# Idle matmuls in TensorE's planned waits, in a planned long convolution and feed-forward kernel

## The chip, the cores and the metric

The kernel runs on one core of one Trainium2 chip. The metric is the device time of one execution in microseconds; the time of a kernel is the median over its runs.

## The reference

The inputs are one batch of 2048 positions with 640 channels. The work is a pre-norm block of two parts: a long convolution (over all 2048 positions, by Fourier transforms) that is gated by the normalised input, and a gated feed-forward of width 1728.

```python
k_shift = sum over t of k_pad[:, t:t + S, :] * shift_k[:, ks - 1 - t]     # 4 taps
kv = k_shift * v
y = irfft(rfft(kv padded to 2S) * rfft(ssm_k padded to 2S))[:S]
y = y + kv * ssm_D
h = x + layernorm(x) * y
h2 = h + (silu(layernorm(h) @ w_gate) * (layernorm(h) @ w_up)) @ w_down
```

`x` is the input `A_q`; all inputs are bfloat16.

## The kernel before

The positions are cut into four blocks `j` of 512. The convolution over 2048 positions becomes block products in a transformed domain: the product for block `j` takes the spectra of value blocks 0 to `j` and of kernel blocks `j` to 0. The channels are cut into two halves `c` of 320. Block 0 uses one dense transform (`dense_c`, line 869): for each of four parts `h` it runs four-step accumulations of 320 columns (`dense_h`), products on VectorE, and eight inverse matmuls into accumulators. Blocks 1 to 3 (`conv_c`, line 1192) use a two-stage transform: `fwd` (line 831) with tables, an SBUF to SBUF shuffle by DMA, `spec` (line 903) with two matmuls of 64 loaded columns[...], products, `inv2`, another shuffle, and a last stage in `conv_bp`. The normalised result is transposed (`ln_bp`, line 1208, matmuls at line 1223) and feeds the feed-forward: `ffn_f` (line 1262) with matmuls of 512 columns, `ffn_b` (line 1284) for the projection down. Transposes of the convolution's kernel are in `k_turn` (line 810), whose first operation is named `ktr00`.

The order of the work is not written by hand. Each operation is an `Op` with a cost per engine; `schedule` (line 255) lays all of them out on a timeline once, in Python, before the program is built. It takes costs from small formulas, such as `mm_c` (line 669) for matmuls and `act_c` and `dve1` for evictions, and priorities from a long list. It also keeps a model of the TensorE clock (`pe_end`, line 180). What it yields for an operation is its engine, its place in the engine's order, and a planned `start` and `finish`. Every operation of an engine is issued in that order.

`emit` (line 367) turns the plan into programs. For each operation it collects the semaphores that it has to wait for, leaves out those already waited for, and appends the waits and then the instructions: "w" is a wait, "f" an instruction without a signal, "i" one with a signal.[...]

PSUM has eight slots of 512 float32 columns[...]: three in the pool `pF` (feed-forward, and in the convolution of block 0 one of the two pairs of accumulators, and some of the taps), five in `pC` (all else). `poolbases` holds their first columns and `seq` the tiles of a pool in the order of the program; a tile's `touch` lists the operations that write or read it, the eviction among them. Evictions are at lines 677 and 680 on ScalarE and lines 678 and 681 on VectorE. Nearly all matmuls are recorded at the helper line 694; VectorE's products and sums are recorded at line 913. Transfers are issued by SyncE (SP) at line 685 and, for accumulating ones, by GpSimd at line 1089.

## Time and profile before

| what | value |
|---|---|
| median of 6 runs | 298.28 us |
| lowest and highest run | 297.25 and 300.76 us |
| time of the profiled execution | 298.61 us |
| its span | 296.8 us |
| mean granted TensorE clock in it | 0.994 |
| TensorE busy | 281.6 us, 95% of the span, 1807 instructions |
| TensorE weight loads busy | 154.2 us, 52%, 1826 instructions |
| VectorE busy | 240.2 us, 81%, 491 instructions |
| ScalarE busy | 196.5 us, 66%, 472 instructions |
| GpSimd busy | 25.7 us, 9%, 31 instructions |

The span is what the hardware profiler saw of the program from the first instruction to the last; the execution's own time is a little longer. Matmuls are pipelined: a record goes on after the next matmul has started, and its end is modelled, so a busy TensorE need not be at its peak. In the 40 slices each digit is the busy share of a slice in tenths, and PEclk is the granted clock in tenths. In the views of waits a line names who waited for whom, then the total in us, the number of times and the longest. In views in order of time a line gives the start and the length in us, then engine, line and operation, how many are merged in it, and in brackets the idle time of the engine ahead of it and what ended it.

### The profile page before, as it was taken

The page shows a single profiled execution, that of the slowest core. Times are in us where ns is not written, and L with a number is a line of the kernel's source. Part 1 is how long each engine was busy: PE and PEld are TensorE (multiplying, and loading weights), DVE is VectorE, ACT ScalarE, POOL GpSimd, SP SyncE. Part 2 cuts the span into 40 slices and gives each one's busy share as a digit, 9 for nine tenths or more (in the row PEclk, how much of TensorE's full clock was granted, in tenths as well). Part 3 has the DMA queues.
Part 4 walks back from the last instruction along what each step waited for, and adds up shares of the span by engine and source line. Part 5 has one row for each costly group of instructions (what it writes and reads, how often), then busy time and mean ns, then how long its engine had stood idle before and what let it go on. Part 6 is the DMA issues. An engine that isn't in the chain of part 4 may idle for free.

```text
span 296.8 us, 5194 instructions
## 1 busy us (share of the span) xinstructions
PE 281.6 (95%) x1807; PEld 154.2 (52%) x1826; DVE 240.2 (81%) x491; ACT 196.5 (66%) x472; POOL 25.7 (9%) x31
## 2 busy tenths in 40 slices
PE   8889988897989999999999999999999999999996
PEld 2466654543534466564444557644444675444574
DVE  4799999999899899999999999994899932304322
ACT  4378899976968968977898995777885131341000
POOL 2000200103111022101101203000010010000000
PEclk9999999799999999999999999999999999999999
DMA  7999997915763787747806007844202033000002
GB/s 220 350 382 315 315 355 253 306 66 156 229 122 114 203 172 215 200 164 177 214 3 176 25 21 200 156 135 154 70 0 79 12 84 93 2 0 0 2 0 88
DMA packets 44050, 43.24 MB, mean 146 GB/s; under 512 B 14895, under 2 KB 38889, under 8 KB 43898
## 3 DMA queue, kind: packets, MB, share of 16 engines
q1 hardware_dynamic: 40168, 38.63, 41.7%
q0 software_dynamic: 3328, 3.97, 8.5%
q10 hardware_dynamic: 530, 0.33, 0.4%
q8 instruction: 14, 0.23, 0.3%
q14 instruction: 10, 0.08, 0.1%
HBM read 20.63 MB, written 2.62 MB: 78 GB/s over the span
## 4 chain that ended last, share of the span: by engine, by line
PE 78%; DVE 15%; DMA 3%; issue 2%; ACT 1%; SPq 1%
PE ps L694 76%; DVE sb L913 12%; DMA sb<-sb 1%; DMA sb<-in_A_q_dram 1%; DVE stt L1003 1%; DVE sb L678 1%; PE ps L1223 1%; SPq L685 1%; ACT sb L677 1%; DVE sb L1028 0%; ACT sb L1249 0%; PE ps L823 0%; DVE sb L681 0%; ACT sb L1042 0%; DVE stt L1007 0%
## 5 line engine op out<-in xcount | busy, mean ns | idle before, releaser
L694 PE MATMUL ps<-sb 128*128 128x320 bf16 (+1 forms) x1207 | 226.2, 339 | 6.3 <-DVE sb L913 2.1
L913 DVE TENSOR_TENSOR sb<-sb 128x1280 bf16<-128x1280 bf16 (+3 forms) x286 | 171.5, 657 | 3.7 <-ACT sb L677 2.7
L694 PEld LDWEIGHTS ps<-sb 128*128 128x128 bf16 (+1 forms) x1226 | 116.4, 98 | 99.5 <-issue 9.6
L677 ACT ACTIVATE sb<-ps 128x320 bf16<-128x320 f32 (+1 forms) x277 | 110.5, 477 | 29.4 <-PE ps L694 22.4
L694 PE MATMUL ps<-sb,tab 128*128 128x320 bf16 (+2 forms) x512 | 64.7, 306 | 5.8 <-issue 1.7
L913 DVE TENSOR_TENSOR sb<-ps,sb 128x512 bf16<-128x512 f32 (+2 forms) x46 | 28.2, 618 | 39.9 <-PE ps L694 28.8
L1249 ACT ACTIVATE sb<-ps 128x512 bf16<-128x512 f32 (+1 forms) x56 | 33.3, 598 | 35.9 <-PE ps L694 35.5
L694 PEld LDWEIGHTS ps<-sb,tab 128*128 128x128 f16 (+2 forms) x512 | 31.7, 101 | 37.5 <-issue 12.4
L1029 ACT ACTIVATE sb<-sb,stt 128x320 bf16<-128x320 bf16 (+1 forms) x27 | 19.6, 761 | 9.3 <-DVE stt L1021 6.6
L1019 POOL TENSOR_TENSOR stt<-stt 128x2 f32<-128x2 f32 (+1 forms) x12 | 12.2, 1024 | 114.5 <-DVE stt L1018 110.1
L1089 POOL DMA_DIRECT2D sb<-sb x12 | 12.2, 1016 | 97.0 <-DVE sb L913 68.5
L680 ACT ACTIVATE sb<-ps 128x320 bf16<-128x320 f32 x46 | 17.6, 449 | 2.6 <-PE ps L694 2.3
L678 DVE CAST sb<-ps 128x320 bf16<-128x320 f32 x32 | 15.0, 479 | 4.5 <-PE ps L694 4.2
L1003 DVE BATCH_NORM_STATS2 stt<-sb 128x6 f32<-128x320 bf16 x32 | 14.3, 474 | 0.1
L1049 ACT ACTIVATE sb<-sb,stt 128x640 bf16<-128x640 bf16 x16 | 13.3, 832 | 0.8 <-DVE stt L1045 0.8
L1042 ACT ACTIVATE sb<-sb 128x640 bf16<-128x640 bf16 x16 | 11.9, 746 | 0.5 <-DMA sb<-in_A_q_dram 0.4
L681 DVE TENSOR_SCALAR sb<-ps 128x320 bf16<-128x320 f32 x10 | 4.8, 484 | 3.5 <-PE ps L694 3.4
L1028 DVE TENSOR_SCALAR sb<-sb,stt 128x320 bf16<-128x320 bf16 (+1 forms) x21 | 7.4, 374 | 0.0
L823 PEld LDWEIGHTS ps<-sb 128*128 128x128 bf16 (+1 forms) x48 | 3.3, 121 | 1.7 <-issue 1.2
L823 PE MATMUL ps<-sb 128*128 128x128 bf16 (+1 forms) x48 | 3.8, 227 | 0.3 <-ACT sb L677 0.3
L1223 PE MATMUL ps<-sb 128*128 128x128 bf16 x40 | 3.8, 243 | 0.0
L1223 PEld LDWEIGHTS ps<-sb 128*128 128x128 bf16 x40 | 3.3, 111 | 0.6
(24 smaller groups left out, 22.7 us busy)
## 6 DMA issues: line engine op xcount, KB each, us to landing
sb<-sb SPq DMA_DIRECT2D x72, 160.0 KB, 2.2
sb<-sb POOLq DMA_DIRECT2D x12, 320.0 KB, 4.4
out_dram<-sb SPq DMA_DIRECT2D x16, 160.0 KB, 2.1
sb<-in_A_k_dram SPq DMA_DIRECT2D x8, 280.0 KB, 4.6
sb<-in_B_w_down_dram SPq DMA_DIRECT2D x13, 160.0 KB, 4.4
sb<-cst_den SPq DMA_DIRECT2D x8, 256.0 KB, 6.6
sb<-in_A_q_dram SPq DMA_DIRECT2D x6, 320.0 KB, 3.7
sb<-in_A_v_dram SPq DMA_DIRECT2D x6, 320.0 KB, 3.4
```

The costliest lines, as they stand in the source:

```text
L677: fns = {"act": lambda a: a.activation(out=dst(), in_=src(), func=ACTF.Copy), "dve": lambda v: v.tensor_copy(out=dst(), in_=src())}
L678: "dve": lambda v: v.tensor_copy(out=dst(), in_=src())}
L680: fns = {"act": lambda a: a.activation(out=dst(), in_=src(), func=ACTF.Copy, scale=scale), "dve": lambda v: v.tensor_scalar(out=dst(), in0 ...
L694: return lambda t: t.matmul(o(), l(), r(), start=st, stop=sp)
L913: return lambda v: v.tensor_tensor(out=o(), in0=a(), in1=b_(), op=op)
L1003: vec(dve1(CW, False), lambda v: v.bn_stats(st6(l, j, b, c), V(xt, b * D + c * CW, CW)), [(xt, (b, c))], [(ST, ("s", l, j, b, c))], prio, ...
L1019: P.op({"pool": 0.75}, lambda g: g.tensor_tensor(out=y, in0=va, in1=stt[:, 420:420 + hi - lo], op=ALU.pow), c1 + [(ST, "half")], c3, prio, ...
L1029: "act": lambda a: a.activation(out=dst(), in_=src(), func=ACTF.Identity, scale=rs(l, j, b), bias=tmv(l, j, 3)[:, b:b + 1])},
L1042: P.op({"act": act_c(D) + 0.22}, lambda a, b=b, jt=jt: a.activation(out=V(jt, 0, D), in_=V(xt, b * D, D), func=ACTF.Copy, accum_out=tmv(l, ...
L1049: P.op({"act": act_c(D) + 0.3}, lambda a, b=b, jt=jt: a.activation(out=V(jt, 0, D), in_=V(xt, b * D, D), func=ACTF.Square, bias=tmv(l, j, ...
L1089: P.op({"pool": 1.35}, [lambda g: g.dma_start(v4(t0), src(), accum_op=ALU.add)], [(t0, 0)] + cells, [(t0, 0)], prio, dma=(2.1, 2.1, 0.8), ...
L1249: P.op({"act": act_c(n)}, lambda a: a.activation(out=dst(), in_=src(), func=ACTF.Silu), rd, wr, -1000, name=f"si{nm}", after=after)
```

## The change

`Prog` gets a new function, `fill`. For an operation `o` of TensorE it looks at the wait that the plan leaves between the end of the operation before, `busy`, and `o.start`. It acts only where the planned start lies between 9 and 62 us and the planned wait is longer than 0.25 us. It goes through all slots of `pF` and `pC`, leaves out a slot whose tile begins with `o`, and takes for the others the tile that was begun last before `o`; from the end of the plan's last operation on that tile (plus 0.14 us) or of `busy`, whichever is later, to `o.start` it counts a free stretch, less 0.12 us. The slot with the longest free stretch is taken, and the number of matmuls is 0.6 of that stretch over 0.0557 us.

`emit` puts the result into TensorE's program ahead of `o`'s own waits: first waits for those operations on the slot's last tile that other engines do, as far as they were not waited for already; then so many matmuls of the 128x128 identity with itself, 128 columns, into the first 128 columns of the slot. Nothing reads what they write, and they signal nothing. It begins after the first operation of `k_turn`. The plan, the order of the operations on every engine, and all transfers stay as they are.

```diff
+    def fill(self, o, busy):
+
+        best = None
+        if 9.0 < o.start < 62.0 and o.start - busy > 0.25:
+            for pn in ("pF", "pC"):
+                for base in self.poolbases[pn]:
+                    ts = [t for t in self.pools[pn].seq if t.base == base and t.touch[0].start < o.start]
+                    prev = max(ts, key=lambda t: t.touch[0].start).touch if ts else []
+                    g = o.start - max([busy] + [p.finish + 0.14 for p in prev]) - 0.12
+                    if any(t.touch[0] is o for t in self.pools[pn].seq if t.base == base):
+                        continue
+                    if g > 0.12 and (best is None or g > best[2]):
+                        best = base, prev, g
+        return best and (best[0], best[1], int(best[2] * 0.6 / 0.0557))
+
     def emit(self, nc, es, block, ndma_sems):
...
+            busy, warm = 0.0, False
             for o in self.order[e]:
                 waits = {}
+                if e == "pe":
+                    fill = self.fill(o, busy) if warm else None
+                    busy, warm = o.finish, warm or o.name == "ktr00"
+                    if fill:
+                        for p in fill[1]:
+                            if p.eng != "pe" and p.semval > seen.get(p.sem.name, 0):
+                                seen[p.sem.name] = p.semval
+                                prog.append(("w", p.sem, p.semval))
+                        prog += [("f", self.filler(fill[0]))] * fill[2]
...
+        P.filler = lambda base: lambda eng: eng.matmul(ps[:, base:base + 128], V(IDN, 0, 128), V(IDN, 0, 128), start=True, stop=True)
```

## Prediction

> **What bounds the kernel now.** I began with the page's slices and with the waits, because the change only adds work to TensorE (PE) and only where PE is planned to be idle.

> ```profile
> PE   8889988897989999999999999999999999999996
> DVE  4799999999899899999999999994899932304322
> PEclk9999999799999999999999999999999999999999
> ```

> One slice is 7.4 us. From slice 3 to slice 9 VectorE (DVE) is full while PE has thin slices; from slice 10 to the end PE is full. The only mark in the clock row is a 7 in the eighth slice. The stage that the change touches ends about there, at the first 512-column matmul of the feed-forward, 60.38 us. Who waits for whom in that stage, PE first, then DVE from 11 to 54 us:

> ```profile
> PE ps L694 <- ACT sb L677: 2.4, 5, 0.8
> PE ps L694 <- DVE sb L913: 2.1, 3, 1.3
> PE ps L694 <- DVE sb L678: 1.6, 3, 1.1
> PE ps L823 <- ACT sb L677: 0.3, 1, 0.3
> ```

> ```profile
> DVE sb L678 <- PE ps L823: 1.3, 1, 1.3
> ```

> PE waits 12 times, 6.4 us in all; DVE waits for PE once, at 10.96 us, at the very start. The chain of waits says the same: from 13.07 to 54.17 us it runs over DVE lines almost alone, and from 54.31 us over PE. So **until 54 us DVE is the bound, and PE's waits there cost nothing by themselves.** Next I cut the stage into the clock's own lengths of 3.41 us (columns: PE busy with its count, PEclk, DMA share, GB/s):

> ```profile
> 13.92:17.33 3.41, 2.07 (x17) 1.00 1.12 367
> 48.05:51.47 3.42, 2.82 (x26) 1.00 0.78 243
> 51.47:54.88 3.41, 1.63 (x17) 1.00 0.98 332
> 54.88:58.29 3.41, 3.41 (x25) 0.50 0.98 295
> 58.29:61.71 3.42, 3.37 (x28) 1.00 0.28 99
> ```

> The window from 51.47 us has the lowest PE share, 1.63 / 3.41 = 48%. The window after it runs at exactly half the clock, and the one after that at full clock. A window with 2.07 / 3.41 = 61% is followed by full clock. So the share that keeps the clock lies between 48% and 61% in this trace. The waits inside the thin window are three of the twelve: 0.62, 0.28 and 1.06 us.

> [...] ten transposes of 128 columns (L1223) from 58.46 us take 0.72 us with a last record of 0.219 us, so (0.72 - 0.22) / 9 = 0.056 us each; halved, (1.27 - 0.31) / 9 = 0.107. [...]

> **The change, part by part.** *How many idle matmuls.* The planned waits are not in the profile; I take the measured ones in their place. A record ends 0.163 us after PE could start the next (299 ns against a 136 ns step), so 6.4 us of idle in 12 waits is 6.4 + 12 x 0.163 = 8.4 us between the streams. The code takes 0.12 us off each: 7.0 us. Times 0.6, over 0.0557: 75 idle matmuls, 75 x 0.056 = 4.2 us of PE. If the plan has half of these waits it is 38, with twice as many 150 (2.1 and 8.4 us); I take 75. Each loads its weights as well (L823: 12 loads in 0.78 us, 0.065 each), beside the matmul before it.

> *What they cost.* At 0.6 of a wait they end before what PE waits for, and then cost nothing: the cover is DVE's work, full from 11 to 54 us. If a real wait is shorter than 0.6 of the planned one, PE starts late by the difference. With all fills exposed it is 4.2 us; with none 0. DVE doesn't wait for PE in that stretch, so a late PE start has first to use up a lead that the profile doesn't tell. I take 0.2 us for some overrun. The added wait on the slot's last reader stands ahead of the fill, so behind it are queued the fill and all of PE; the reader is an eviction planned to be over, in a slot not used since. I take 0, bounds 0 and the 0.5 us of one eviction (L677, 477 ns).

> *Does the clock stay up?* In the thin window the three waits are 0.62 + 0.28 + 1.06, plus 3 x 0.163, less 3 x 0.12, that is 2.1 us, and 0.6 of it 1.26 us. Busy becomes 1.63 + 1.26 = 2.9 of 3.41, 85%. Even a third of it (0.42) gives 2.05, 60%, near the share that was enough. So I take the halving as gone.

> *What that is worth.* Extra streaming in the halved window: pairs of 64-column loads step by 0.240 instead of 0.135 us, 4.5 pairs, 0.47; three 320-column matmuls 0.267, 0.241 and 0.216 instead of 0.136, 0.32; ten transposes 0.107 instead of 0.056, 0.51. Sum 1.3 us, the most it can give here. But not all of it lies on the path: DVE is full there too. The last five transposes at 58.74 us need a normalised row block that DVE starts at 58.12 and ends at 58.56 us, and DVE itself had only about 0.1 us of waits on PE between 54.8 and 58 us. Those five can come forward by about 0.1 us, and the feed-forward with them; with DVE's own waits 0.2 us. That is the lower end in *this* execution. In others, if the window lies about a microsecond later or stays halved for two windows, the halved stretch covers the PE-full stretch from 58.74 us, and the loss is the 1.3 us or a little more. Between 0.2 and 1.3 I take 0.8; less 0.2 of overrun: **0.6 us**.

> *Does it arrive at the end?* After 60.38 us PE streams until 70.80 and then waits 1.49 us. The instructions' records show that this matmul waits for the landing of the last of nine transfers that SP issues between these times:

> ```profile
> 63.11 6.44 SPq L685 DMA_DIRECT2D sb<-sb  x9
> 72.28 1.37 SPq L760 DMA_TRANSPOSE sb<-in_A_ssm_k_dram  x1
> ```

> The first seven land 2.2 to 2.4 us after issue; the one issued at 68.20 us lands at 72.20, 4.0 us later, because GpSimd's accumulating transfer, issued at 67.88 us, is under way until 72.01. Those issues follow ScalarE's evictions, and so PE. If PE is early, SP is early, and the wait ends early with it. DVE runs dry right after, which shows that nothing else holds the end there:

> ```profile
> 75.20 0.49 DVE L681 TENSOR_SCALAR sb<-ps 128x320 bf16<-128x320 f32 x1 [1.59 <-PE ps L694]
> ```

> From 84 us on the chain is PE with few breaks, so what is gained by then is kept. Sum against the profiled execution: its time is 298.61 us, its span 296.8, 1.8 us around it unchanged; 298.61 - 0.6 = 298.0. That execution is 0.33 us above the median of six, 298.28; the forecast for the median is 298.28 - 0.6 = **297.7 us**.

> **The rivals.** *B, the gain is multiplied at the shuffle (faster).* If the last shuffle gets its packets in ahead of the GpSimd transfer, it lands after 2.4 us instead of 4.0; the 1.49 us of PE go with it, and so do the 1.59 us of DVE. For it: six transfers just before were not slowed, and 0.3 us between the two issues decide. Against it: DVE, which starts the GpSimd transfer, comes a little forward too. 297.7 - 1.5 = 296.2 us.

> *C, the fills overrun (slower).* Place: the short waits from 38 to 54 us, where PE's input comes straight from ScalarE's eviction (five of the waits) and DVE casts PE's output (L678). If the plan has waits where the chip has none, the fills go in front of work that DVE needs next. Price: 4.2 us if all is exposed; if the plan and the chip disagree on half of them, 2.1 us, which DVE no longer hides once PE's lead over it is used up. It decides from the point at which a fill exceeds its real wait by more than that lead. Less 0.3 us for the clock: 298.28 + 1.8 = 300.1 us. Against it: DVE has only one wait on PE in 43 us, and a fill takes 0.6 of a wait.

> *D, no effect.* The fills miss the thin window, because the plan has its waits elsewhere, or do not count as activity; the clock is halved as before, and DVE hides the rest: 298.3 us.

> **How the numbers follow.** Chances: forecast 0.36, B 0.31, C 0.21, D 0.12. About 0.5% (1.5 us) is what a measurement of this kernel can tell from no change. The forecast lies within it, D too; B lies beyond it at 0.7%, C beyond it at 0.6%. Of the forecast I give 0.03 to more than 0.5% faster, and 0.02 of B stays within: faster 0.32, same 0.47, slower 0.21. The range goes from B's time less 0.3 (the upper end of the clock's worth added) to 299.9 us, short of most of C: 295.9 to 299.9 us. The forecast's own range is 297.0 to 298.3 us.

> **What would show it.** Right: about 75 new 128-column matmuls before 62 us; a busy PE share above 61% in each 3.41 us window; a granted clock of 1.00 from 10.5 us to the end of the work; DVE still without waits on PE until 54 us; the feed-forward's first 512-column matmul between 59.1 and 60.2 us. B: the PE wait near 70.8 us under 0.5 us. C: new waits of DVE or ScalarE on PE between 11 and 54 us, and the first 512-column matmul later than 60.4 us. D: a clock of 0.50 again for 3.41 us. The forecast is wrong if the halved clock was worth more than 1.3 us to the executions that the median counts, or if the fills stand where PE does not wait.

## The result and the profile after

The changed kernel takes 301.27 us (median of 21 runs, 299.56 to 304.39) against 298.33 us (42 runs) for the kernel before on the same chips: ratio **1.0101, 95% interval 1.0081 to 1.0122, slower by 1.0%**. The forecast was 297.7 us with a range to 299.9. The time lies above that range. Ratios here leave out the few executions that ran more than 1.5% above the fastest one of their kernel, so a ratio can differ a little from that of the two medians.

The profiled execution of the changed kernel has a span of 300.6 us (before: 296.8). Its slices, as in the prediction:

```profile
PE   8999999796999999999999999999999999999996
DVE  4899999898599998999999999895799942304322
PEclk9999999999799999999999999999999999999999
```

What the change does to TensorE by itself is what was meant. There are 70 idle matmuls, called fills below (75 were estimated). PE's waits on other engines before 62 us shrink, from 6.4 us in 12 waits to 3.5 us in 9:

```profile
PE ps L719 <- DMA sb<-sb: 1.3, 1, 1.3
PE ps L719 <- DVE sb L938: 0.9, 3, 0.4
PE ps L1248 <- DVE sb L1053: 0.4, 1, 0.4
PE ps L719 <- ACT sb L702: 0.4, 2, 0.2
PE ps L719 <- DVE sb L703: 0.3, 1, 0.3
PE ps L848 <- ACT sb L702: 0.2, 1, 0.2
```

(Lines are numbered 25 higher than before; the idle matmuls have line 1375.) But the first row has a new cause. It is the wait that took 1.06 us at 54.31 us before and ended then with an eviction of VectorE (line 678). Now that eviction is over at 53.95 us, and PE waits on for a shuffle that lands at 54.86 us.

And the clock is not halved at 54.85 us any more, but at 74.84 us, after a new thin window. In each of the two traces the changes of the clock lie whole numbers of 3.41 us apart (before: 10.47 and 54.85 us, 13 lengths; after: 9.99 and 74.84 us, 19 lengths), but they start from another place in each execution. So the windows of this execution are not those of the prediction, and are laid out from its own changes:

```profile
50.95:54.36 3.41, 2.32 (x29) 1.00 0.94 338
54.36:57.77 3.41, 2.66 (x25) 1.00 0.91 246
...
71.42:74.84 3.42, 0.95 (x7) 1.00 0.40 107
74.84:78.26 3.42, 3.42 (x15) 0.50 0.58 144
```

The first of these rows is the lowest between 10 and 62 us: 2.32 / 3.41 is 68%, and full clock followed.

**Where the time came from.** VectorE runs the same 491 instructions in the same order in both kernels, so each can be set beside its twin. Up to 54 us the changed kernel is not late at all: the pairs of 64-column loads that start at 52.51 us before start at 52.29. The lateness then comes in steps: +0.59 us at VectorE's eviction that started at 54.81 us before, +3.19 at 75.20, +2.48 at 85.59, +2.00 at 100.26, +3.15 at 116.67, +3.78 at 186.83 and to the end. The first, the second and the last of the four rises end at a wait of PE for a shuffle, the third at a wait of VectorE for a load. In order of time on SP's queue around the second one (start, length of the issuing stretch):

```profile
63.54 7.97 SPq L710 DMA_DIRECT2D sb<-sb  x9
73.88 1.37 SPq L785 DMA_TRANSPOSE sb<-in_A_ssm_k_dram  x1
```

The same nine shuffles took 6.44 us to issue before. The chain of work that ended last runs through them in the changed kernel (start and length in us; SPq is an issue by SP):

```profile
65.64 0.59 SPq L710
66.23 0.04 issue
66.27 1.79 SPq L710
68.06 0.04 issue
68.10 0.61 SPq L710
68.71 0.04 issue
68.75 4.86 DMA sb<-sb
73.61 0.28 issue
73.89 8.48 PE ps L719 x45
```

The instruction records give the reason for the difference: the issue at 66.27 us holds SP for 1.79 us instead of 0.61, and three shuffles issued from 65.01 us on land after 4.0, 3.8 and 3.6 us instead of 2.2. Of the shuffles that PE's next matmul needs (the eighth is the last of them, not the ninth as the prediction has it), two are then issued behind GpSimd's accumulating transfer instead of one. What waits for them, PE and then DVE:

```profile
PE ps L719 <- DMA sb<-sb: 2.7, 1, 2.7
```

```profile
78.39 0.49 DVE L706 TENSOR_SCALAR sb<-ps 128x320 bf16<-128x320 f32 x1 [4.35 <-PE ps L719]
```

PE waits 2.65 us instead of 1.49; that makes the thin window (busy for 0.95 of 3.41 us), and the halved clock after it (0.50 for 3.41 us) stretches PE's next part: five 512-column matmuls from 75.36 us take 2.34 us instead of 1.24. DVE runs dry for 4.35 us instead of 1.59.

No transfer was added or moved by the change. What was added is instructions, and the queue table has a row for those, which I passed over. In the page of before and then of after:

```profile
q8 instruction: 14, 0.23, 0.3%
```

```profile
q8 instruction: 15, 0.25, 0.3%
```

The packet records of the trace show what these are: single packets of 16,384 bytes, each under way for 0.9 to 1.5 us, and between two of them TensorE goes through 251 recorded instructions on average (before; matmuls, loads and a few waits). I take them for fetches of TensorE's program, and the instructions between two of them for a block; the runs below that only add TensorE instructions move them too (one from 80.71 us to 77.49 with 28 more). An idle matmul is two instructions in the records, a load and a matmul; 70 of them are 140 (3731 records of TensorE before, 3871 after), over half of 251. The 14 fetches of before have all come earlier, by 3.6 to 14.5 us, and there is a 15th. Before, fetches were at 59.68 us, when SP issued nothing, and at 80.71, beside a shuffle whose issue took 2.32 us: the kernel before pays for a meeting too. After, they are at **52.50 and 66.19 us**, each while SP issues a train of shuffles: those are the two first steps of the lateness. At the first of them, four shuffles issued from 50.37 us on land after 3.9 to 4.5 us; before, issued from 50.60 us on, after 2.8 to 3.0. The third and the fourth follow fetches at 109.56 and 187.07 us, beside shuffles whose issue took 1.71 and 1.27 us.

### The profile page after: what moved, and what is told of

The parts are those of the page before. It is cut to its first block, busy times and chain, and to the rows that moved or that the text cites. A ratio compares the mean times of both kernels' runs of the same rounds, so it can differ in the third digit from the quotient of the medians.

```text
span 300.6 us, 5334 instructions
## 1 busy us (share of the span) xinstructions
PE 286.2 (95%) x1877; PEld 157.9 (53%) x1896; DVE 240.1 (80%) x491; ACT 196.6 (65%) x472; POOL 25.7 (9%) x31
## 4 chain that ended last, share of the span: by engine, by line
PE 71%; DMA 8%; DVE 8%; ACT 5%; SPq 4%; issue 2%
PE ps L719 70%; DVE sb L938 6%; DMA sb<-sb 5%; SPq L710 4%; ACT sb L702 3%; DMA sb<-in_A_k_dram 2%; DMA sb<-in_A_q_dram 1%; DVE sb L703 1%; ACT sb L1274 1%; ACT sb L705 1%; PE ps L848 1%; DVE sb L1053 0%; ACT sb L1067 0%; PE ps L1248 0%; DVE sb L753 0%
## 5 line engine op out<-in xcount | busy, mean ns | idle before, releaser
L719 PEld LDWEIGHTS ps<-sb 128*128 128x128 bf16 (+1 forms) x1226 | 116.6, 99 | 97.9 <-issue 10.5
L1114 POOL DMA_DIRECT2D sb<-sb x12 | 12.2, 1016 | 99.5 <-DVE sb L938 72.8
L1375 PE MATMUL ps<-sb 128*128 128x128 bf16 x70 | 5.6, 220 | 0.0
L1375 PEld LDWEIGHTS ps<-sb 128*128 128x128 bf16 x70 | 4.5, 98 | 0.9 <-issue 0.4
L1248 PE MATMUL ps<-sb 128*128 128x128 bf16 x40 | 3.6, 220 | 0.4 <-DVE sb L1053 0.4
```

The source lines that it names most:

```text
L719: return lambda t: t.matmul(o(), l(), r(), start=st, stop=sp)
L1114: P.op({"pool": 1.35}, [lambda g: g.dma_start(v4(t0), src(), accum_op=ALU.add)], [(t0, 0)] + cells, [(t0, 0)], prio, dma=(2.1, 2.1, 0.8), ...
```

## The experiments

Three theories went in. **F**: the shifted fetches delay the transfers that SP issues. **T**: the fills cost TensorE time, or start its work late (rival C of the prediction). **K**: the fills move the halved clock from a covered place to an exposed one. All ratios are to the kernel before on the same chip, with their 95% intervals; its medians were 298.40 us in the first four and 298.32 us in the last four. Each group of four shared one chip.

### Fills without columns

```diff
-  eng.matmul(ps[:, base:base + 128], V(IDN, 0, 128), V(IDN, 0, 128), start=True, stop=True)
+  eng.matmul(ps[:, base:base + 8], V(IDN, 0, 128), V(IDN, 0, 8), start=True, stop=True)
```

> The same 70 idle matmuls at the same places, but of 8 columns, so nearly no TensorE time and no activity to speak of; the number of instructions is that of the changed kernel. Theory F (the 140 added TensorE instructions bring the 16 KB instruction fetches of TensorE earlier, and these meet the shuffles that SP issues): about as slow as the changed kernel, 299.8 to 302.0 us, with fetches at 52 to 53 us and near 66 us. Theory T (the fills cost TensorE time, or late starts behind them): as before, 297.5 to 299.0 us. Theory K (the fills keep the clock up at 55 us and the halving then falls where it costs more): as before, 297.5 to 299.0 us, and the clock is halved near 55 us again.

Measured: 301.84 us, ratio 1.0089 (1.0062 to 1.0117). As slow as the changed kernel. In the trace these fills step by 25 ns, 1.8 us in all, and the clock is halved from 55.94 us, about where it was before (and here also from 8.16 us, for two lengths). So neither the fills' time nor a moved halving is needed for the loss. The fetches are at 51.56 and 66.56 us, an SP issue at 66.61 us takes 2.15 us, and the nine shuffles stretch again:

```profile
63.88 8.31 SPq L710 DMA_DIRECT2D sb<-sb  x9
74.23 1.37 SPq L785 DMA_TRANSPOSE sb<-in_A_ssm_k_dram  x1
```

T and K fail here, except for one part of T: these fills still have the added waits on their slots' readers ahead of them. That those cost nothing is shown only by the kernel that is a whole block longer, below.

### The same idle time in fewer instructions

```diff
-  return best and (best[0], best[1], int(best[2] * 0.6 / 0.0557))
+  return best and (best[0], best[1], int(best[2] * 0.6 / 0.2157 + 0.5))
...
-  eng.matmul(ps[:, base:base + 128], V(IDN, 0, 128), V(IDN, 0, 128), start=True, stop=True)
+  eng.matmul(ps[:, base:base + 512], V(IDN, 0, 128), V(TAPS, 0, 512), start=True, stop=True)
```

> The same idle TensorE time in a quarter of the instructions: matmuls of 512 columns (identity times the tap rows), the number rounded to the nearest, some 18 of them, so about 36 instructions more than before in place of 140. Theory F: the fetches come only about 2 us earlier than before (near 57 and 78 us), and the time is 296.5 to 299.0 us. Theory T: as the changed kernel or slower, 300.5 to 302.5 us. Theory K: as the changed kernel, 300.5 to 302.0 us.

Measured: 300.00 us, ratio 1.0031 (1.0007 to 1.0055), with 18 fills and a full clock throughout. Between the expectations; F's number missed it as well. The fetch at 77.46 us meets SP at 77.62 us (1.16 us for the issue of a load that takes 0.43 before), and a shuffle issued at 76.41 us lands after 3.33 us instead of 2.50. SP waits for that landing and begins its next train of shuffles at 79.83 us instead of 79.08; PE's wait at 84.73 us grows to 1.39 us, where it was 0.91. I had expected little from a shift of 2 us; "early by little" isn't "harmless".

### More instructions without any fill

```diff
-  pe([mm(... B32(pt, 0, 512), ... V(WD, 12 * D, 512), True, True) for _ in range(2)], 512, 2,
+  pe([mm(... B32(pt, 0, 128, o=x * 128), ... V(WD, 12 * D, 128), True, True) for _ in range(2) for x in range(4)], 512, 2,
```

> The kernel before, without fills; each of the 14 warm-up matmuls of 512 columns at the start is cut into four of 128 columns, so TensorE does the same columns with 84 instructions more, all of them before 10 us. Theory F: from 20 us on every fetch comes about a third of a block (5 to 7 us) earlier, near 54 and 75 us, and the time moves by more than 0.3% without any fill, by my guess to 299.0 to 301.0 us. Theories T and K: as before, 297.7 to 298.9 us.

Measured: 296.95 us, ratio 0.9951 (0.9927 to 0.9976): **faster**. The kernel before has become 0.5% faster by nothing but 84 instructions more in its warm-up. That the time moves is what F says and T and K exclude; the direction I had wrong. Its fetches are at 57.92 and 75.36 us, none of them near 80.7 us, where the kernel before had its long issue. PE's waits for a shuffle or for no cause shown, from 62 to 100 us, before and then here:

```profile
PE ps L694 <- issue: 1.5, 1, 1.5
PE ps L694 <- DMA sb<-sb: 0.9, 1, 0.9
```

```profile
PE ps L694 <- issue: 1.4, 1, 1.4
```

The first line is in both kernels the wait near 71 us that the prediction traced to a shuffle. The second, at 83.7 us, is gone, and VectorE, 0.3 us early until then, is 1.06 us early at its operation of 85.59 us.

### Fills and more instructions

The changed kernel with the diff just shown.

> The changed kernel with the same cutting of the warm-up matmuls: 84 + 140 = 224 instructions more than before[...]. Theory F: from 60 us on the fetches stand within 3 us of those of the kernel before, shifted by one block, and the time comes back to 297.0 to 299.5 us with all 70 fills in place. Theories T and K: as the changed kernel, 300.5 to 302.0 us.

Measured: 299.09 us, ratio 1.0020 (0.9994 to 1.0046). All 70 fills are there, and most of the loss is gone. Fetches at 59.31 and 80.12 us, within 0.6 us of those of the kernel before; the next, at 104.38 us, comes 4.1 us later than there.

### A whole block more

The same with the eight matmuls that spread the taps cut in three, for 256 instructions more than before, my estimate of a block from the 251 recorded between two fetches:

```diff
...
-  pe([mm(lambda: B32(pt, 0, CW), lambda: V(ONE, 0, 128, 0, 1), rhs, True, True)], CW, 2,
+  cut = [(0, 107), (107, 107), (214, 106)]
+  pe([mm(lambda o=o, n=n: B32(pt, 0, n, o=o), lambda: V(ONE, 0, 128, 0, 1), lambda o=o, n=n: rhs(o, n), True, True) for o, n in cut], CW, 2,
```

> The changed kernel with all 70 fills, the warm-up matmuls cut into four (84 instructions more) and each of the 8 matmuls that spread the taps cut into three (32 more): 84 + 140 + 32 = 256 instructions more than before[...], so after the last fill the fetches stand where they stand in the kernel before. Theory F: the loss of the changed kernel is gone with every fill in place, ratio 0.997 to 1.002 (297.5 to 299.0 us); what differs from the kernel before is then what the fills themselves are worth. Theories T and K: ratio 1.008 to 1.012, as the changed kernel.

Measured: 298.30 us, ratio **1.0011 (0.9986 to 1.0035)**. With every fill in place and the program one block longer, the kernel is as fast as before. Fetches at 59.38 and 80.46 us (before: 59.68 and 80.71), and the shuffles issue in 6.44 us again:

```profile
63.19 6.44 SPq L710 DMA_DIRECT2D sb<-sb  x9
72.29 1.37 SPq L786 DMA_TRANSPOSE sb<-in_A_ssm_k_dram  x1
```

This is the test that only F passes. It also tells what the fills are worth by themselves, the clock included: nothing that these runs can tell from zero.

The execution that was profiled is the slowest of the 22, 301.19 us. Until 143 us its VectorE is never more than 0.25 us behind that of the kernel before; its 2.6 us are lost between 143 and 151 us. The fetch ahead of that stands at 134.09 us (before: 134.18), the shuffle's issue beside it takes 1.93 us (before: 1.53), and PE then waits 1.6 us for a shuffle. So the same place of a fetch doesn't settle the time of every single execution. That the loss is gone is a statement about the medians.

### A ninth of a block more, without fills

Each warm-up matmul cut in two: 28 instructions more.

> The kernel before without fills, each warm-up matmul cut into two: 28 instructions more, a ninth of a block. Theory F: fetches about 2 us earlier, near 57.5 and 78.5 us as with the wide fills, and a time near that of the wide fills, 299.0 to 300.5 us. Theories T and K: as before, 297.8 to 299.0 us.

Measured: 300.48 us, ratio 1.0068 (1.0038 to 1.0099), as F expected. The fetch near 60 us is at 60.37 us, later than before and not earlier as F said. The next is at 77.49 us, as with the wide fills, and PE's waits from 62 to 100 us show the same new size of the last shuffle wait (second line; 0.9 us before):

```profile
PE ps L694 <- issue: 1.8, 2, 1.4
PE ps L694 <- DMA sb<-sb: 1.3, 1, 1.3
```

So the wide fills' loss needs no fill to explain it: 28 instructions without one do as much or more.

### 112 instructions more, without fills

Warm-up matmuls cut in four, six of the tap matmuls in three and two in two.

> The kernel before without fills, the warm-up matmuls cut into four and the tap matmuls into two or three: 112 instructions more. Theory F: fetches about 8 us earlier than before, near 55 and 72 us; by my guess near the kernel with 84, 296.5 to 299.0 us, and in any case not the time of the kernel before by rule. Theories T and K: as before, 297.8 to 299.0 us.

Measured: 298.28 us, ratio 1.0013 (0.9986 to 1.0040). Within F's range, but also within T's and K's, so it decides nothing. Its fetches at 56.12 and 67.98 us do meet SP's work (a load with an issue of 1.85 us and a shuffle with 1.38), and PE's wait at 72.8 us is 1.78 us. VectorE is then 0.49 us late at its operation of 75.20 us, but 0.25 us early at that of 85.59 us, as nothing meets SP where the kernel before has its fetch at 80.71 us.

### Wide fills at the good place

18 wide fills (36 instructions) and 8 warm-up matmuls cut in four (48), 84 in all.

> The 18 wide fills of 512 columns (36 instructions) and 8 of the 14 warm-up matmuls cut into four (48): 84 instructions more, as in the fastest kernel so far, and the clock kept up as well. Theory F: fetches from 54 us on as in that kernel, ratio 0.992 to 0.997 (295.8 to 297.3 us), some 0.3% below it if the halved clock was worth about a microsecond. Theory T: as the wide fills alone, 299.5 to 300.5 us.

Measured: 296.65 us (295.65 to 296.89), ratio **0.9924 (0.9901 to 0.9947)**, the fastest of all, faster than both kernels of this study. From 62 to 100 us PE has no wait left near 84 us; the first line is the wait near 71 us again:

```profile
PE ps L719 <- issue: 1.4, 1, 1.4
PE ps L719 <- ACT sb L702: 0.2, 1, 0.2
```

Its interval overlaps that of the 84 instructions without fills, and these two ran on different occasions; whether the fills add to it stays open.

All in one table. Fetches are those between 50 and 85 us; "long issue" is the longest time that one issue held SP beside the second of them (undisturbed, a shuffle takes about 0.6 us; in the rows of 28 and of 18 it is a load, 0.43 us before). Fetches and issues are those of one execution, ratios those of many:

| kernel | instructions added | fetches, us | long issue, us | ratio |
|---|---|---|---|---|
| before | 0 | 59.68, 80.71 | 2.32 | 1 |
| whole block, 70 fills | 256 | 59.38, 80.46 | 1.61 | 1.0011 |
| 84 + 70 fills | 224 | 59.31, 80.12 | 1.17 | 1.0020 |
| 28, no fills | 28 | 60.37, 77.49 | 1.22 | 1.0068 |
| 18 wide fills | 36 | 58.17, 77.46 | 1.16 | 1.0031 |
| 84, no fills | 84 | 57.92, 75.36 | 0.72 | 0.9951 |
| 84 with 18 wide fills | 84 | 58.38, 75.91 | 0.84 | 0.9924 |
| 112, no fills | 112 | 56.12, 67.98 | 1.38 | 1.0013 |
| changed kernel | 140 | 52.50, 66.19 | 1.79 | 1.0101 |
| 70 fills of 8 columns | 140 | 51.56, 66.56 | 2.15 | 1.0089 |

Kernels whose fetches stand alike are alike in time, fills or not. The number of fills and the width of them order nothing.

The ten traces together tell more of the meetings. Of 504 shuffles issued with no fetch's packet within 0.1 us and no transfer of GpSimd under way, none held SP for more than 0.67 us. With a transfer of GpSimd alone under way, 27 of 300 shuffles took more than 0.9 us to issue, at most 1.38. With a fetch and no transfer of GpSimd it was 12 of 55, at most 1.79; that longest one is the issue at 66.27 us in the changed kernel. The cases beside a fetch differ by whether SP was at work: in 22 of them SP was already issuing when the packet began, and the next issue, a shuffle, began while the packet was under way; that issue took 0.81 to 2.32 us in every case. Where SP was not issuing when the packet began, 17 of 19 took at most 0.78 us.

## Why the prediction was wrong, point by point

- **What bounds the kernel until 54 us: right.** DVE has no new wait on PE before 54 us, and no instruction of PE up to 52.3 us is late.
- **How many idle matmuls: right in size**, 75 against 70.
- **What they cost in TensorE time: right to take little.** I took 0.2 us for overrun; measured 0 before 54 us. Rival C came nearest to the measured time (300.1 us against 301.27) by a mechanism that did not occur: its first sign, new waits of DVE or ScalarE on PE between 11 and 54 us, did not come. Its second, a first 512-column matmul later than 60.4 us, came (60.81 us), but through the shuffle that landed at 54.86 us. That C was near is luck.
- **Does the clock stay up: right at 55 us.** The lowest share before 62 us was 68%, above the 61% that I asked for. The clock fell later (0.50 at 74.84 us), after the wait of 2.65 us for a shuffle.
- **What that is worth, 0.8 us: wrong.** That other executions have the halved stretch elsewhere was an assumption of mine; the changed kernel's trace has it at 74.84 us, that of the 8-column fills at 55.94. Over the executions of the kernel before in the first four comparisons the mean clock and the span tell how many halved stretches of 3.41 us there were. With none the median is 298.45 us (11 executions), with one 298.30 (29), with two 297.71 (20); in the last four comparisons 298.26 (6), 298.22 (28) and 298.59 (14). A halved stretch costs nothing that shows in this count, which doesn't tell where each stretch fell; DVE's cover, which I had put at the lower end only, holds. The whole-block kernel says the same.
- **Does it arrive at the end: the place was right, the sign wrong.** The wait behind the nine shuffles was the sensitive point, as rival B said, but it grew, from 1.49 to 2.65 us.
- **The step that failed** is the cost of the added instructions: "with all fills exposed it is 4.2 us; with none 0". It priced them as time on TensorE and put at nothing, without a reason, that each is also 2 instructions more in TensorE's program, and that the fetches come earlier with them (59.68 to 52.50 us, 80.71 to 66.19). The runs put that term at about 2.7 us (an estimate: the ratio falls from 1.0101 to 1.0011 with the fetches put back, 0.9% of 298.3 us), a loss, where the forecast had a gain of 0.6 us in all. The row for it was on the page, with 0.3% of the engines' time. A share that small says nothing of a packet beside which a train of nine shuffles takes 7.97 us to issue instead of 6.44, just where PE and DVE wait for it.

What stays open: how a fetch and a long issue of SP hang together. The trace shows the packet (at 66.19 us) and the long issue beside it (1.79 us at 66.27), but not how the one acts on the other. Where a transfer of GpSimd is under way too, the two are not separated. I did not separate how much of the changed kernel's loss is the halved clock at 74.84 us, which follows from the longer DMA wait in that execution. With 8-column fills and no halved clock there, VectorE's lateness grows by 1.2 us at that place (0.78 to 1.96), in the changed kernel by 2.8 (0.43 to 3.19); the 1.6 us between them is an estimate for that one execution. In the median the two kernels are alike.

## What to carry to other kernels

In this kernel an instruction of TensorE had a second price, its place in the program: 28 added ones moved a fetch from 80.71 to 77.49 us, 84 to 75.36, and that alone was worth +0.7% and -0.5%, without any change of the work, as PE waits here for transfers of 160 KB. Before a small gain or loss of another kernel is put down to an edit, look in its trace where the packets of the instruction row stand. Where the edit has moved them, pad the engine's program, with the added instructions ahead of the stretch that matters, until they stand where they stood (256 TensorE instructions did it here, within 0.3 us), and measure again; if the effect goes, it was the fetches. Few instructions are no protection: 28 cost 0.7% here, 112 nothing that shows.
